# Spreading an expert's routing over more units, and placing its list matmuls one quarter later

## The chip, the cores and the metric

The kernel runs on one core of a Trainium2 chip. The metric is the time of one execution on the device in microseconds (us); the kernel before takes 2542.33 us, the median of three runs (2541.45 to 2545.57).

## What is computed

Two layers follow each other. The first is an attention without softmax over 8 batches of 2496 rows; the second is a mixture of 8 experts over all 19968 rows, where each row goes to one expert and each expert takes exactly 2496 rows.

```python
# attention, per batch: u, v of 2496 x 256, z of 2496 x 64
attn = np.maximum(scale * (z @ z.T), 0.0) ** 2
x = u * (attn @ v)
# mixture of experts over all rows of x
logits = x @ w_gate                      # 19968 x 8
for (token, expert) in the order of falling logits:
    if token is free and expert has under 2496 tokens: assign it
out[token] = relu(x[token] @ w1[expert]) @ w2[expert]
```

The greedy assignment is the part that the change touches. The kernel does it expert by expert: it finds the expert that fills first and the logit at which it is full (a search over thresholds), closes that expert, and goes on with the rest.

## The kernel before

The attention takes about the first 1490 us and is written in an order of its own; the change doesn't touch it. The rest is `moe`, whose order is that in which the program emits its instructions: each engine gets them as a list, and the framework's scheduler interleaves them by priority of emission and by the costs that it assumes.

The experts run one after the other. An expert's 2496 tokens are cut into five groups of up to 512, and the hidden width of 1024 into eight chunks of 128, so there are 8 x 5 x 8 = 320 steps. Step n emits the second layer of chunk n (`layer2`, twelve matmuls of 256 columns, lines L621 to L623) and the first layer of chunk n + 3 (`layer1`, six matmuls of up to 512 columns, L590 to L592). Each product of 32-bit numbers is made of three matmuls on high and low parts, so ScalarE makes the high part hh of the hidden chunk (L609) and VectorE the low part hl (L610). Weights are split in the same way (w1l and w2l, L510), and so are the tokens: they are gathered by GpSimd (L481), laid out through DRAM, transposed on VectorE (xt, L549) and split (xh on ScalarE, L553; xl on VectorE, L554).

While expert k - 1 computes, `route(k)` finds the tokens of expert k. It is a generator whose `yield`s carry weights ("units"), about 102 in sum for one routing, and `advance`, called twice a step (80 times per expert), draws as many units as the line with `YIELDS` wants; at the last call of an expert all that is left is drawn. So `YIELDS` sets how evenly the routing's instructions are spread among the matmuls of 40 steps.

A routing has these parts. The logits of the closed expert are shut and the best open expert of each row is found again (L69 to L91). Then come two searches of six rounds: VectorE compares all keys with up to seven thresholds (`mask`, L97), ten matmuls count them per expert (`srch`, L240), VectorE reduces the counts (hd L244, hr L246, hx L247), one matmul spreads them to all partitions (L323), VectorE picks the threshold (best L325, Dg L330, T L301, V L312) and makes the next mask. A last histogram with the mask fmask ends in L353. Then the ranks of the expert's tokens are made: running counts (cum, tot L376), a matmul over partitions (L388), rank and rj (L390 to L410). Last the list: for each quarter of 40 columns VectorE makes one-hot tiles (oa L420, hl L423 twice, and four ob tiles L429, which are queued behind the fourth last hl by `behind(4)`), and 40 matmuls of 40 columns each put the token numbers in place (L435; 36 in the last quarter). From the result VectorE makes idx (L440), the list that the gathers and the scatters of that expert use. The eighth expert takes what is left and has no search.

Of the kernel before, what the change touches and what calls it, by code (L numbers as in the profile page):

```python
# [21 lines left out]
def tile_attention_then_moe(ctx, tc, u, v, z, w_gate, w1, w2, out):  # L22
# [41 lines left out]

    attention(tc, u, v, z, w_gate, xd, identf, made, first, 1.0 / S)
    moe(tc, xd, first, jp, identf, w1, w2, out, B, S, consts, dram)


# [39 lines left out]
def moe(tc, xd, first, jp, identf, w1, w2, out, B, S, cp, dram):  # L108
    nc = tc.nc
# [3 lines left out]
    KT = NT + 1  # L113
# [3 lines left out]
    J = B * NT + B // 2  # L117
# [10 lines left out]
    ND = 15  # L128
    LA = 3
    AHEAD = 12  # L130
    YIELDS = 88
    with ExitStack() as ctx:
        rp = ctx.enter_context(tc.tile_pool(name="rp", bufs=1))
        wp = ctx.enter_context(tc.tile_pool(name="wp", bufs=3))
# [77 lines left out]
        CB = JP // 4  # L212
        QW = 4
# [5 lines left out]
        def by_quad(row, n):  # L219
            return row.rearrange("p (q r) -> p q r", r=QW)[:, :, None, :].to_broadcast([128, QN, n, QW])  # L220
# [9 lines left out]
        def srch():  # L230
            return ps.tile([128, 512], F32, name="srch")
# [20 lines left out]

        def behind(lag):
            return tc.issue_after(paced[-lag].ins) if len(paced) >= lag else nullcontext()

        def route(k):
            if k:
# [28 lines left out]
            else:  # L286
# [6 lines left out]
                for stage in range(2):  # L293
                    V = floor
                    for r, w in enumerate(widths):
                        n = (1 << w) - 1
# [24 lines left out]
                        p = srch()  # L321
# [29 lines left out]
                p = srch()  # L351
# [35 lines left out]
            p = srch()  # L387
# [25 lines left out]
            ROUTE[k]["idx"] = idx  # L413
            if k:
                p = srch()
                for c in range(0, JP, CB):
                    q = slice(c, c + CB)
                    oa = rp.tile([128, QN, KT, QW], BF, name="oa", bufs=2)
                    hl = rp.tile([128, QN, 2, KT, QW], BF, name="hl", bufs=2)
                    nc.vector.tensor_tensor(oa, by_quad(rab[:, 0, q], KT),  # L420
                                            slot[:, None, :KT].to_broadcast([128, QN, KT, QW]), op=OP.is_equal)
                    for i, d in enumerate((idh, idl)):
                        nc.vector.tensor_mul(hl[:, :, i], oa, by_quad(d[:, q], KT))  # L423
                    yield 1.5
                    ob = rp.tile([128, QN, 128, QW], BF, name="ob", bufs=4)
                    for b in range(0, 128, 32):
                        z = b + 32
                        with behind(4):
                            nc.vector.tensor_tensor(ob[:, :, b:z], by_quad(rab[:, 1, q], z - b),  # L429
                                                    slot[:, None, b:z].to_broadcast([128, QN, z - b, QW]),  # L430
                                                    op=OP.is_equal)
                        yield 1.5
                    for j in range(c, min(J, c + CB)):
                        n, r = divmod(j - c, QW)
                        nc.tensor.matmul(p[:, :2 * KT], ob[:, n, :, r], hl[:, n, :, :, r],  # L435
                                         start=(j == 0), stop=(j == J - 1))
                    yield
                idl_f = rp.tile([128, KT], F32, name="idl_f")
                nc.vector.tensor_copy(idl_f, p[:, KT:2 * KT])
                nc.vector.scalar_tensor_tensor(idx, p[:, :KT], 128.0, idl_f, op0=OP.mult, op1=OP.add)  # L440
                yield
                return
            both = [rp.tile([128, QN, 128, QW], BF, name="ob", bufs=4) for c in range(0, JP, CB)]
            for a0, a1 in ((0, 8), (8, 2 * KT)):
                na = a1 - a0
                p = srch()
                for c in range(0, JP, CB):
                    q = slice(c, c + CB)
                    ob = both[c // CB][:, :, :64]
                    hl = both[c // CB][:, :, 64:64 + 2 * na].rearrange("p q (i a) r -> p q i a r", i=2)  # L450
# [10 lines left out]
                    for j in range(c, min(J, c + CB)):  # L461
                        n, r = divmod(j - c, QW)
                        nc.tensor.matmul(p[:64, :2 * na], ob[:, n, :, r], hl[:, n, :, :, r],  # L463
                                         start=(j == 0), stop=(j == J - 1))
# [202 lines left out]
        for k in range(E):  # L667
# [13 lines left out]
            for h in range(2):  # L681
                at(n0 - 10 + h, split_w, k, 1, 0, h)
                at(n0 - 8 + h, split_w, k, 2, 0, h)
                at(n0 - 4 + h if k else -1, split_w, k, 1, 1, h)
                at(n0 - 2 + h if k else h, split_w, k, 2, 1, h)
        head = route(0)
        for mark in head:
            if mark == "listed":
                break
        N = len(seq)  # L690
        done = 0
        steps_k = {k: 0 for k in range(E)}
        gens = {k: route(k) for k in range(1, E)}

        def advance(pos):
# [4 lines left out]
            if pos < skip:  # L700
                return
            want = -(-(pos % (2 * PER) - skip + 1) * YIELDS // (2 * PER - skip))
            if (pos + 1) % (2 * PER) == 0:
# [406 lines left out]
```

## Time and profile before

| | |
|---|---|
| median of three runs | 2542.33 us (2541.45 to 2545.57) |
| profiled execution, its own time | 2541.26 us |
| its span | 2539.5 us |
| TensorE busy | 2445.5 us, 96% |
| VectorE busy | 1983.8 us, 78% |
| ScalarE busy | 1480.0 us, 58% |
| mean granted clock of TensorE | 0.977 |

The span is that of the profiled execution alone; its own time lies 1.07 us below the median. A line number in the profile is a line of the kernel above. PE is TensorE, DVE VectorE, ACT ScalarE, POOL GpSimd. In a group of instructions the last column is the idle time of the engine just before them, with the engines that ended it.

### The profile page before, as it was taken

The numbers are of one execution on the slowest core, as the hardware profiler recorded it, in microseconds if no ns is written. First come the engines' busy times: TensorE is split into PE (matmuls) and PEld (weight loads), VectorE is DVE, ScalarE is ACT, GpSimd is POOL, SyncE is SP. The second block draws the span as 40 slices with busy tenths as digits, with TensorE's granted clock in tenths as the row PEclk, the third lists the DMA queues.
The fourth block names the chain that finished last, engine by engine and source line by source line (L and its number), as shares of the span: only waits on it lengthen the run. The fifth ranks groups of instructions, "written<-read, shape, count | busy, mean of one in ns | idle before, by whom it ended". The sixth has DMA issues, their size and how long they took to land.

```text
span 2539.5 us, 67151 instructions
## 1 busy us (share of the span) xinstructions
PE 2445.5 (96%) x27913; PEld 2270.1 (89%) x27913; DVE 1983.8 (78%) x5653; ACT 1480.0 (58%) x1837; POOL 384.4 (15%) x747
## 2 busy tenths in 40 slices
PE   8999999999999999999999489999999999999998
PEld 7999999999999999999999377888888988898997
DVE  7888888888888988888877676979696968796332
ACT  7887888888887888888876022333333333333332
POOL 0000000000000000000000022423333233333331
PEclk9999999999999999999999578999999999999999
DMA  6031131121311311311100013332333232334320
GB/s 167 19 89 43 35 96 35 38 77 35 81 51 35 81 34 43 88 35 44 42 19 19 9 57 82 111 116 79 89 96 100 86 106 89 105 106 124 100 71 24
DMA packets 220705, 174.74 MB, mean 69 GB/s; under 512 B 167152, under 2 KB 188656, under 8 KB 220400
## 3 DMA queue, kind: packets, MB, share of 16 engines
q1 hardware_dynamic: 205296, 129.54, 18.1%
q0 software_dynamic: 15104, 40.91, 5.3%
q8 instruction: 218, 3.57, 0.6%
q14 instruction: 87, 0.71, 0.1%
HBM read 110.11 MB, written 60.29 MB: 67 GB/s over the span
## 4 chain that ended last, share of the span: by engine, by line
PE 86%; DVE 8%; issue 2%; DMA 1%; ACT 1%; POOL 1%; another core or an unknown queue 0%; SPq 0%; POOLq 0%; DVEq 0%; ACTq 0%
PE acc L927 43%; PE sc L856 11%; PE y L621 5%; PE y L623 5%; PE y L622 5%; PE hp L590 5%; PE hp L591 5%; PE hp L592 4%; PE srch L240 2%; PE srch L435 1%; DVE ob L429 1%; PE srch L463 1%; DVE mask L97 1%; POOL xg L481 1%; DMA wr<-in_moe_w_dram 0%
## 5 line engine op out<-in xcount | busy, mean ns | idle before, releaser
L927 PE MATMUL acc<-vh,hi 64*128 64x256 f32 x5280 | 744.7, 280 | 1.2 <-POOL seen L933 0.8
L927 PE MATMUL acc<-vl,hi 64*128 64x256 f32 x5280 | 740.9, 279 | 0.0
L927 PE MATMUL acc<-vh,lo 64*128 64x256 f32 x5016 | 709.4, 279 | 0.1
L877 DVE TENSOR_TENSOR lo<-a,hi 128x1024 fp32r<-128x1024 f32 (+3 forms) x400 | 457.3, 1143 | 103.6 <-ACT hi L869 102.8
L927 PEld LDWEIGHTS acc<-vh,hi 64*128 64x128 f32 x5280 | 502.0, 187 | 23.3 <-POOL seen L933 7.1
L609 ACT ACTIVATE hh<-hp 128x512 fp32r<-128x512 f32 (+1 forms) x320 | 186.9, 587 | 555.3 <-PE hp L592 429.0
L862 ACT ACTIVATE a<-sc 128x1024 f32<-128x1024 f32 (+1 forms) x400 | 400.1, 1000 | 178.5 <-PE sc L856 141.3
L927 PEld LDWEIGHTS acc<-vl,hi 64*128 64x128 f32 x5280 | 502.4, 187 | 0.0
L927 PEld LDWEIGHTS acc<-vh,lo 64*128 64x128 f32 x5016 | 477.5, 187 | 12.2 <-DVE lo L877 0.8
L963 DVE SCALAR_TENSOR_TENSOR lt<-xs,wgb 128x256 bf16<-128x256 f32 x1248 | 473.1, 421 | 1.4
L863 ACT ACTIVATE a<-a 128x1024 f32<-128x1024 f32 (+1 forms) x400 | 416.0, 1040 | 12.7
L621 PE MATMUL y<-w2h,hh 128*128 128x256 f32 (+1 forms) x1280 | 366.5, 286 | 2.3 <-ACT hh L609 1.9
L622 PE MATMUL y<-w2l,hh 128*128 128x256 f32 (+1 forms) x1280 | 363.4, 284 | 0.0
L869 ACT ACTIVATE hi<-a 128x1024 fp32r<-128x1024 f32 (+1 forms) x248 | 258.0, 1040 | 6.7
L590 PE MATMUL hp<-xh,w1h 128*128 128x512 f32 (+2 forms) x646 | 258.2, 402 | 3.6 <-ACT xh L583 1.6
L591 PE MATMUL hp<-xl,w1h 128*128 128x512 f32 (+2 forms) x646 | 254.0, 393 | 0.3 <-issue 0.3
L621 PEld LDWEIGHTS y<-w2h,hh 128*128 128x128 f32 (+1 forms) x1280 | 241.4, 189 | 13.1 <-ACT hh L609 2.4
L592 PE MATMUL hp<-xh,w1l 128*128 128x512 f32 (+2 forms) x646 | 250.0, 388 | 0.0
L622 PEld LDWEIGHTS y<-w2l,hh 128*128 128x128 f32 (+1 forms) x1280 | 241.4, 189 | 8.7
L933 POOL MEMSET seen<- 1x1 f32 x400 | 42.4, 106 | 1350.7 <-PE acc L927 1350.7
L653 POOL DMA_INDIRECT out_dram<-y,idx x160 | 173.1, 1082 | 383.9 <-ACT y L648 328.0
L481 POOL DMA_INDIRECT xg<-xd,idx x160 | 165.0, 1031 | 404.9 <-issue 110.3
(1162 smaller groups left out, 4055.7 us busy)
## 6 DMA issues: line engine op xcount, KB each, us to landing
vr<-in_v_dram SPq DMA_DIRECT2D x32, 512.0 KB
ur<-in_u_dram SPq DMA_DIRECT2D x32, 512.0 KB
xd<-xs SPq DMA_DIRECT2D x32, 512.0 KB
wr<-in_moe_w_dram SPq DMA_DIRECT2D x32, 512.0 KB
xgd<-xg SPq DMA_DIRECT2D x30, 512.0 KB
xg<-xgd SPq DMA_DIRECT2D x120, 128.0 KB
zw<-in_z_dram SPq DMA_DIRECT2D x112, 76.0 KB
xg<-xgd SPq DMA_DIRECT2D x32, 112.0 KB
```

The source lines that it names most:

```text
L590: nc.tensor.matmul(p[:, c], wh, xh, start=(d == 0), stop=False)
L591: nc.tensor.matmul(p[:, c], wh, xl, start=False, stop=False)
L592: nc.tensor.matmul(p[:, c], wl, xh, start=False, stop=(d == DH - 1))
L621: nc.tensor.matmul(o, h[:, c], wh, start=first, stop=False, skip_group_check=True)
L622: nc.tensor.matmul(o, h[:, c], wl, start=False, stop=False, skip_group_check=True)
L856: nc.tensor.matmul(P[s][:, t], x[b][r, k * 128:(k + 1) * 128], y[b][r, g * 512:g * 512 + w], start=(i == 0), stop=(i == 2))
L862: nc.scalar.activation(A[s], p, AF.Relu, scale=scale)
L863: nc.scalar.activation(A[s], A[s], AF.Square)
L869: nc.scalar.activation(HI[s], A[s], AF.Copy)
L877: nc.vector.tensor_sub(LO[s][:, :n], a[:, :n], h[:, :n].bitcast(F32))
L927: mm = nc.tensor.matmul(o, p, q, start=(kt == run == i == k == 0), stop=(last and k == 1), skip_group_check=True)
L963: nc.vector.scalar_tensor_tensor(t[r], XS[b, g][r, i], 1.0, WG["rows"][r, e], op0=OP.mult, op1=OP.mult, accum_out=lg[r, j, e:e + 1])
```

## The change

`YIELDS` goes from 88 to 96. The list matmuls of a quarter move into a function `place`, and are emitted only when the one-hot tiles of the next quarter have been; the last quarter's come after one more yield of 1.5 units. The number of instructions stays as it is.

```diff
--- before.py
+++ after.py
@@ -128,7 +128,7 @@
     ND = 15
     LA = 3
     AHEAD = 12
-    YIELDS = 88
+    YIELDS = 96
     with ExitStack() as ctx:
         rp = ctx.enter_context(tc.tile_pool(name="rp", bufs=1))
         wp = ctx.enter_context(tc.tile_pool(name="wp", bufs=3))
@@ -252,6 +252,12 @@
 
         def behind(lag):
             return tc.issue_after(paced[-lag].ins) if len(paced) >= lag else nullcontext()
+
+        def place(p, c, ob, hl):
+            for j in range(c, min(J, c + CB)):
+                n, r = divmod(j - c, QW)
+                nc.tensor.matmul(p[:, :2 * KT], ob[:, n, :, r], hl[:, n, :, :, r],
+                                 start=(j == 0), stop=(j == J - 1))
 
         def route(k):
             if k:
@@ -413,6 +419,7 @@
             ROUTE[k]["idx"] = idx
             if k:
                 p = srch()
+                ready = []
                 for c in range(0, JP, CB):
                     q = slice(c, c + CB)
                     oa = rp.tile([128, QN, KT, QW], BF, name="oa", bufs=2)
@@ -430,11 +437,12 @@
                                                     slot[:, None, b:z].to_broadcast([128, QN, z - b, QW]),
                                                     op=OP.is_equal)
                         yield 1.5
-                    for j in range(c, min(J, c + CB)):
-                        n, r = divmod(j - c, QW)
-                        nc.tensor.matmul(p[:, :2 * KT], ob[:, n, :, r], hl[:, n, :, :, r],
-                                         start=(j == 0), stop=(j == J - 1))
-                    yield
+                    ready.append((c, ob, hl))
+                    if len(ready) == 2:
+                        place(p, *ready.pop(0))
+                yield 1.5
+                place(p, *ready.pop(0))
+                yield
                 idl_f = rp.tile([128, KT], F32, name="idl_f")
                 nc.vector.tensor_copy(idl_f, p[:, KT:2 * KT])
                 nc.vector.scalar_tensor_tensor(idx, p[:, :KT], 128.0, idl_f, op0=OP.mult, op1=OP.add)
```

The lines behind the change shift: what is L323 before is L329 in the kernel after, L376 is L382, L429 is L436, L435 is L259 in `place`, L510 is L518, L590 to L592 are L598 to L600, L610 is L618, L621 to L623 are L629 to L631.

**The list on VectorE.** Here stands the start of the fourth expert's list in VectorE's row before (oa, ob and the list's hl are the one-hot tiles; hl__ with a number is a step's low part):

```order
L610 SCALAR_TENSOR_TENSOR hl__35317<-hp,hh 128x512
L420 TENSOR_TENSOR oa<-rab,slot 128x800
L429 TENSOR_TENSOR ob<-rab,slot 128x10x128
L423 TENSOR_TENSOR hl<-oa,idh 128x10x80
L423 TENSOR_TENSOR hl<-oa,idl 128x10x80
L610 SCALAR_TENSOR_TENSOR hl__35355<-hp,hh 128x512
L429 TENSOR_TENSOR ob<-rab,slot 128x10x128 x3
L610 SCALAR_TENSOR_TENSOR hl__35390<-hp,hh 128x512
L420 TENSOR_TENSOR oa<-rab,slot 128x800
L429 TENSOR_TENSOR ob<-rab,slot 128x10x128
L423 TENSOR_TENSOR hl<-oa,idh 128x10x80
L423 TENSOR_TENSOR hl<-oa,idl 128x10x80
```

And after:

```order
L427 TENSOR_TENSOR oa<-rab,slot 128x800
L618 SCALAR_TENSOR_TENSOR hl__35278<-hp,hh 128x512
L430 TENSOR_TENSOR hl<-oa,idh 128x10x80
L430 TENSOR_TENSOR hl<-oa,idl 128x10x80
L436 TENSOR_TENSOR ob<-rab,slot 128x10x128 x2
L618 SCALAR_TENSOR_TENSOR hl__35303<-hp,hh 128x512
L436 TENSOR_TENSOR ob<-rab,slot 128x10x128 x2
L427 TENSOR_TENSOR oa<-rab,slot 128x800
L618 SCALAR_TENSOR_TENSOR hl__35328<-hp,hh 128x512
L430 TENSOR_TENSOR hl<-oa,idh 128x10x80
L430 TENSOR_TENSOR hl<-oa,idl 128x10x80
L436 TENSOR_TENSOR ob<-rab,slot 128x10x128
```

The first oa now stands ahead of a low part, where it stood behind one, and the four ob tiles of the first quarter stand in two pairs with a low part between them, where one stood alone and three together.

**The first round of a search.** In VectorE's row of the fifth routing, from the first mask on, before:

```order
L97 TENSOR_TENSOR mask<-rep,at_28082 128x1120
L510 TENSOR_TENSOR w1l<-wr,w1h 128x512
L610 SCALAR_TENSOR_TENSOR hl__35969<-hp,hh 128x448
L510 TENSOR_TENSOR w1l<-wr,w1h 128x512
L244 TENSOR_TENSOR hd<-srch,diag 128x7x16
L246 TENSOR_REDUCE hr<-hd 128x7
L247 TENSOR_TENSOR hx<-hr,dE 128x8x7
L325 SCALAR_TENSOR_TENSOR best<-srch,step_28074 128x8x7
L330 TENSOR_REDUCE Dg<-best 128x1
L610 SCALAR_TENSOR_TENSOR hl__36009<-hp,hh 128x448
L301 TENSOR_TENSOR T<-next_28084,Dg 128x7
L312 TENSOR_TENSOR V<-floor,Dg 128x1
```

After:

```order
L97 TENSOR_TENSOR mask<-rep,at_28082 128x1120
L618 SCALAR_TENSOR_TENSOR hl__35884<-hp,hh 128x448
L618 SCALAR_TENSOR_TENSOR hl__35933<-hp,hh 128x448
L518 TENSOR_TENSOR w1l<-wr,w1h 128x512
L618 SCALAR_TENSOR_TENSOR hl__35969<-hp,hh 128x448
L244 TENSOR_TENSOR hd<-srch,diag 128x7x16
L518 TENSOR_TENSOR w1l<-wr,w1h 128x512
L246 TENSOR_REDUCE hr<-hd 128x7
L247 TENSOR_TENSOR hx<-hr,dE 128x8x7
L331 SCALAR_TENSOR_TENSOR best<-srch,step_28074 128x8x7
L336 TENSOR_REDUCE Dg<-best 128x1
L618 SCALAR_TENSOR_TENSOR hl__36019<-hp,hh 128x448
```

The mask stands two low parts earlier, one of the two w1l stands between hd and hr instead of before hd, and the low part between Dg and T is a later one.

On TensorE, the same place, from the last of the ten histogram matmuls to L323, before:

```order
L240 MATMUL srch<-mask,oh 128x112
L590 MATMUL hp<-xh_35659,w1h 128x448
L591 MATMUL hp<-xl_35660,w1h 128x448
L592 MATMUL hp<-xh_35659,w1l 128x448
L590 MATMUL hp<-xh_35782,w1h 128x448
L591 MATMUL hp<-xl_35783,w1h 128x448
L592 MATMUL hp<-xh_35782,w1l 128x448
L323 MATMUL srch<-hx,onesr 128x64
```

And after, the last matmuls in front of what is now L329 (the twelve matmuls of a second layer, of which these are the last two, stand between them and the histogram):

```order
L630 MATMUL y_35944<-w2l,hh 64x256
L631 MATMUL y_35944<-w2h,hl__35884 64x256
L598 MATMUL hp<-xh_35672,w1h 128x448
L599 MATMUL hp<-xl_35673,w1h 128x448
L600 MATMUL hp<-xh_35672,w1l 128x448
L598 MATMUL hp<-xh_35782,w1h 128x448
L599 MATMUL hp<-xl_35783,w1h 128x448
L600 MATMUL hp<-xh_35782,w1l 128x448
L329 MATMUL srch<-hx,onesr 128x64
```

Between the histogram and the matmul that spreads the counts there were six matmuls of a first layer, and now there are those six and twelve of a second layer.

**The last routing.** VectorE's row of the eighth expert's routing, from the selection of its tokens to the offsets that L388's result gives, before:

```order
L367 TENSOR_SCALAR sel<-asg,cstar 128x160
L510 TENSOR_TENSOR w1l<-wr,w1h 128x512
L371 SCALAR_TENSOR_TENSOR cum<-ones_j,sel 128x160
L610 SCALAR_TENSOR_TENSOR hl__39576<-hp,hh 128x448
L376 CAST tot<-cum 128x1
L510 TENSOR_TENSOR w1l<-wr,w1h 128x512
L390 TENSOR_SCALAR off<-srch 128x1
```

After:

```order
L373 TENSOR_SCALAR sel<-asg,cstar 128x160
L377 SCALAR_TENSOR_TENSOR cum<-ones_j,sel 128x160
L618 SCALAR_TENSOR_TENSOR hl__39460<-hp,hh 128x448
L382 CAST tot<-cum 128x1
L618 SCALAR_TENSOR_TENSOR hl__39509<-hp,hh 128x448
L518 TENSOR_TENSOR w1l<-wr,w1h 128x512
L618 SCALAR_TENSOR_TENSOR hl__39576<-hp,hh 128x448
L396 TENSOR_SCALAR off<-srch 128x1
```

The running count tot stands two low parts earlier, and in front of the w1l instead of behind one.

## Rows read from the trace of the kernel before

**Rows 1.** The page: busy time by engine, and the clock row of the 40 slices.

```profile
PE 2445.5 (96%) x27913; PEld 2270.1 (89%) x27913; DVE 1983.8 (78%) x5653; ACT 1480.0 (58%) x1837; POOL 384.4 (15%) x747
...
PEclk9999999999999999999999578999999999999999
```

**Rows 2.** TensorE's groups, 1530 to 2540 us; last column idle time before, with its releasers.

```profile
L435 PE MATMUL srch<-hl,ob 128*128 128x40 bf16 x1092 | 48.9, 214 | 0.0
...
L240 PE MATMUL srch<-mask,oh 128*128 128x112 bf16 (+1 forms) x710 | 41.9, 205 | 7.2 <-DVE mask L97 6.1 <-issue 0.9
L323 PE MATMUL srch<-hx,onesr 128*128 128x64 f32 (+1 forms) x71 | 15.2, 213 | 8.0 <-DVE hr L246 3.6 <-DVE hx L247 3.6
...
L353 PE MATMUL srch<-hx,onesr 128*128 128x16 f32 x6 | 1.4, 235 | 1.7 <-DVE hr L246 0.9 <-DVE hx L247 0.8
```

**Rows 3.** The same view, 1620 to 1712 us (routing of the second expert).

```profile
L240 PE MATMUL srch<-mask,oh 128*128 128x112 bf16 (+1 forms) x120 | 7.0, 204 | 1.4 <-issue 0.9 <-DVE mask L97 0.2
L323 PE MATMUL srch<-hx,onesr 128*128 128x64 f32 (+1 forms) x12 | 2.5, 209 | 1.6 <-DVE hx L247 1.5
```

**Rows 4.** The same view, 1742 to 1845 us (routing of the third expert).

```profile
L240 PE MATMUL srch<-mask,oh 128*128 128x112 bf16 (+1 forms) x120 | 7.0, 204 | 1.6 <-DVE mask L97 1.6
L323 PE MATMUL srch<-hx,onesr 128*128 128x64 f32 (+1 forms) x12 | 2.7, 221 | 2.3 <-DVE hr L246 1.2 <-DVE hx L247 0.9
```

**Rows 5.** The same view, 2005 to 2105 us (routing of the fifth expert).

```profile
L240 PE MATMUL srch<-mask,oh 128*128 128x112 bf16 (+1 forms) x120 | 7.0, 204 | 1.3 <-DVE mask L97 1.3
L323 PE MATMUL srch<-hx,onesr 128*128 128x64 f32 (+1 forms) x12 | 2.4, 202 | 1.3 <-DVE hx L247 1.2
```

**Rows 6.** Timeline, 1563 to 1569 us: start, duration, engine, line, operation, idle before.

```profile
1563.11 0.67 PE L240 MATMUL srch<-mask,oh 128*128 128x112 bf16 x10
...
1563.59 0.36 PE L621 MATMUL y<-w2h,hh 128*128 128x256 f32 x1
...
1564.03 0.28 PE L621 MATMUL y<-w2h,hh 128*128 128x256 f32 x1
...
1564.39 0.40 PE L590 MATMUL hp<-xh,w1h 128*128 128x512 f32 x1
...
1564.45 0.22 DVE L247 TENSOR_TENSOR hx<-hr,dE 128x56 fp32r<-128x56 f32 x1
...
1564.62 0.40 PE L591 MATMUL hp<-xl,w1h 128*128 128x512 f32 x1
...
1564.86 0.22 PE L323 MATMUL srch<-hx,onesr 128*128 128x64 f32 x1
...
1565.82 0.83 DVE L97 TENSOR_TENSOR mask<-rep,T 128x1120 bf16<-128x1120 int16 x1
...
1566.70 0.67 PE L240 MATMUL srch<-mask,oh 128*128 128x112 bf16 x10
...
1566.82 0.69 DVE L610 SCALAR_TENSOR_TENSOR hl__29736<-hp,hh 128x512 fp32r<-128x512 f32 x1
```

**Rows 7.** The same view, 2019 to 2023.5 us (a first round).

```profile
2021.02 1.06 DVE L510 TENSOR_TENSOR w1l<-wr,w1h 128x512 fp32r<-128x512 f32 x1
...
2022.61 0.22 DVE L247 TENSOR_TENSOR hx<-hr,dE 128x56 fp32r<-128x56 f32 x1
2022.88 0.30 PE L323 MATMUL srch<-hx,onesr 128*128 128x64 f32 x1 [1.22 <-DVE hx L247]
```

**Rows 8.** VectorE's groups, 1530 to 2540 us.

```profile
L549 DVE STREAM_TRANSPOSE xt<-xg 128x512 f32<-128x512 f32 (+1 forms) x76 | 52.6, 692 | 0.4
```

**Rows 9.** TensorE's waits, 2265 to 2340 us: total, times, longest.

```profile
PE hp L590 <- ACT xh L553: 1.3, 1, 1.3
PE srch L388 <- issue: 0.9, 1, 0.9
```

**Rows 10.** Windows: length, busy time of each engine, granted clock, DMA share, GB/s.

```profile
2292.00:2296.00 4.00, 3.31 (x46) 2.86 (x47) 4.00 (x8) 2.77 (x4) 0.94 (x1) 0.82 0.44 120
2296.00:2300.00 4.00, 4.00 (x20) 3.54 (x20) 2.18 (x4) 0.60 (x1) 3.08 (x4) 0.75 0.46 117
```

## The prediction

> **What bounds the kernel now.** I read the page first. TensorE is busy 2445.5 us of a span of 2539.5, and the clock row is at full speed but for the hand-over between the two halves [rows 1]. The second half, from about 1490 us, is where the change lies. So I grouped TensorE's instructions there by line, from 1530 us to 2540 us: the reader is to look at the last column, the idle time in front of each group. The list matmuls L435, which the change moves, waited 0.0 us in 1092 instructions. The search waits: 7.2 us before the histograms L240, 8.0 before L323, 1.7 before L353 [rows 2]. The rest is small. So all that an order of emission can win there is about 20 us, 0.8% of the time, and most of it is the search's chain between VectorE and TensorE, six times over (the eighth expert is found without a search).
>
> Then the same view per routing: the second expert's search loses 1.4 + 1.6 us [rows 3], the third's 1.6 + 2.3 [rows 4], the fifth's 1.3 + 1.3 [rows 5]. With 0.3 each for L353 these are 3.3, 4.2 and 2.9. Of the total of 16.9 that leaves 6.5 for the first, fourth and sixth searches. The fourth and sixth have the same order of instructions as the fifth, so they take about 2.9 each and the first about 0.7.
>
> Last the timeline of one round that stands clear [rows 6]: L240 starts at 1563.11, VectorE's hx at 1564.45 is ready for L323 at 1564.86, the next mask starts at 1565.82 and its histogram at 1566.70. L240 itself takes TensorE 0.48 (the next matmul starts at 1563.59). So TensorE needs some 1.2 us of other matmuls between a histogram and L323 (1564.86 less 1563.11 is 1.75, less the 0.48, less a little slack), and some 1.7 between L323 and the next histogram (1.84 less L323's own 0.06 and slack), or it waits. I call the matmul work that stands there the cover, counted from the order at 0.12 us per 256-column and 0.23 per 512-column matmul (1564.03, 1564.39, 1564.62: three spacings of the one, then one of the other). A foreign VectorE instruction inside the chain adds its own time: hl 0.69 [rows 6], a transpose xt 0.69 [rows 8], a w1l 1.06 [rows 7].
>
> **The change part by part.** (a) It removes and adds no instruction on any engine: 0.
>
> (b) The list matmuls stand later against VectorE's one-hot tiles. They waited 0.0 before [rows 2], so nothing can be won there. The last quarter still stands where it stood in TensorE's order, so the token list and the gathers behind it come no earlier either: 0. What changes is the slot of everything else: at 96 units the routing is spread more evenly, about 6 of its 102 units are left for the last call instead of 15, and VectorE takes up the list and the next search two to three steps (2.84 us each) sooner.
>
> (c) The first routing keeps its order up to the list: 0.
>
> (d) Routings 4, 5 and 6, alike. First round: VectorE had two w1l in front of hd, the second from 2021.02 to 2022.08, so hx came at 2022.61 and L323 waited 1.22 [rows 7] behind a cover of 1.23. Afterwards 18 matmuls stand there instead of 6 (cover 2.66), and the mask is issued two steps earlier; one w1l stays between hd and hr. Chain 1.2 + 1.06 + some 0.5 of an hl in front is 2.8 against 2.66: 0.2 stays of 1.2, so -1.0. Second round: the next mask is queued behind an hl half a step ahead, the need is 1.7 + 0.69 = 2.4, and the cover falls from 2.66 to 2.04: +0.5 (0.4 and a late start). In the eighth round an xt (0.69) is now in a chain with cover 2.13, against 1.2 + 0.69 = 1.9, where the cover was 2.83 before: between 0 and 0.7, taken as +0.3. In the twelfth, an hl and an xt (1.38) against the same 2.13: 2.6 less 2.13, +0.4. The other rounds lose or gain 0.1 to 1.5 us of cover, most of them without falling below the need; the third, fourth and ninth rounds, fmask's histogram and L353 together I put at +0.6, bounded by -0.4 (all hold) and +1.4 (each 0.3 late). Sum +0.8 per routing; three of them +2.4. The bounds: -1.8 per routing if only 1.1 of the 2.9 stays, +3.2 if every hl that stands in a chain is late.
>
> (e) Routing 2: the 1.4 at the first histogram stays, since VectorE is still full there. The L323 that stood with no cover waited 1.5 of the 1.6 [rows 3]; it gets a cover. As in (d) about 0.7 comes new in other rounds: -0.8.
>
> (f) Routing 3: the first round as in (d) and its L323 waits of 2.3 [rows 4] go down by 1.4; the second mask adds 0.5: -0.9.
>
> (g) Routing 8, the last, has two waits of TensorE, 0.9 at L388 and 1.3 at the first matmul of a new block of rows, which waits for xh [rows 9]. The running count tot had a w1l (1.06) and an hl in front of it; afterwards its w1l stands behind, and the transpose for xh is one step (2.84 us) earlier in VectorE's row. Both waits are shorter than these shifts: -0.9 and -1.3. Behind the second wait the granted clock was 0.82 and then 0.75 for 4 us each [rows 10], at full speed before. The work lost is (0.18 + 0.25) x 4 = 1.7 us, and it goes with the waits: -1.7. Nothing is late next there, since the last routing has no search behind it. If the transposes' data land late instead, 0 of the 3.9.
>
> A rule that speaks against this reading is weighed here. The row shows a granted clock that stayed at full speed through waits of 1.2 us and more in the searches, as before L323 [rows 7], and fell only at the last routing. The Trainium skill's page "TensorE: Matmul & The Clock Gate", in "HAM oscillation — how this bites in real kernels", says that the gate falls back to its low rate over gaps in which TensorE waits, and that the price is paid again at each gap; by it, new waits close together in three searches would each cost clock as well. That is rival D below.
>
> Sum: 0 + 0 + 0 + 2.4 - 0.8 - 0.9 - 3.9 = -3.2 us. The profiled execution took 2541.26 us and lies 1.1 us below the median of the runs shown, 2542.33. 2541.3 - 3.2 is 2538.1, and in the median's frame **2539.1 us**.
>
> **The rivals.** A, faster: VectorE's lead of two to three steps covers the rounds of (d) as well, so that hl's are done before the masks fall due. For it: the whole loss of (d) hangs on foreign instructions that stand in the chain by issue order, and an instruction that was issued early and done early costs nothing. Against it: VectorE's hl can't run before ScalarE and TensorE have made its input, whatever its lead. Then each of three routings wins 1.0 instead of losing 0.8: 5.4 less, **2533.7**.
>
> B, no gain at the end: in the last routing the row block lands late by its DMAs, not by VectorE, and 0.9 + 1.3 + 1.7 = 3.9 stay. For it: the first wait reads as issue, not as VectorE [rows 9]. **2543.0**.
>
> C, slower: the half-step lead with which the hl's now stand in front of masks and hd makes VectorE wait in order for TensorE's next layer-1 matmul at about six places of a search, 0.4 us more each than I gave, in routings 3 to 6: 6 x 0.4 x 4 = 9.6, **2548.7**. For it: VectorE takes its row in order, and a mask behind an hl can't pass it. Against it: five rounds of the old order stand so already, and the fifth routing lost 2.9 in all [rows 5]. It decides from 2.1 us more per routing on (8.3 to the bound of slower, in four).
>
> D, the clock: what the last routing shows, 1.7 us of lost work behind two waits [rows 9, 10], happens in four searches: 6.8 more, **2545.9**. Against it: the waits of before, of like length, cost no clock.
>
> That the change does nothing is no rival, since the order on VectorE and TensorE moves in six of seven routings; that gains and losses cancel lies within the likeliest case's own range.
>
> **How the numbers follow.** The forecast has 0.50 (its own range 2536.5 to 2542.0), A 0.22, B 0.15, C 0.10, D 0.03. A measurement of this kernel can tell about 0.2%, 5.1 us: faster is below 2537.2, slower above 2547.4. Faster: A's 0.22 and about a quarter of the forecast's half, 0.12: 0.34. Slower: C's 0.10 and the upper ends of D and B, 0.02: 0.12. The rest, 0.54, is no difference. The range goes from 2533.0, a little below A, to 2546.5, above B and D; what is left out is C, some 0.1, and A's lower half, under 0.1.
>
> **What would show it.** In the changed kernel: list matmuls still without idle time; the first L323 of routings 4 to 6 with 0.3 us or less in place of 1.22; 0.3 to 0.7 us at the second histogram of each of them; 3.5 to 4 us of search waits in each; no wait at L388 and none at the xh block in the last routing, and a clock at full speed through it. Searches that lose under 2 us each speak for A, a clock still at 0.75 in the last routing for B, 5 us or more each for C. The forecast is wrong if the search's idle time of the second half (16.9 us now) comes out under 15 or over 20, or if anything outside these seven routings moves.

## The result, and the profile after

The kernel after takes 2561.67 us (median of four runs, 2556.9 to 2564.07), the kernel before 2541.89 on the same chip: a ratio of 1.0077 [1.0059, 1.0095]. It is slower by 19.8 us, where 3.2 us faster was forecast. The profiled execution took 2560.87 us, span 2559.1, which is 19.6 us over that of before. The page, lines as in [rows 1]:

```profile
PE 2450.8 (96%) x27913; PEld 2268.6 (89%) x27913; DVE 1979.8 (77%) x5653; ACT 1480.0 (58%) x1837; POOL 379.7 (15%) x747
...
PEclk9999999999999999999999579999999999999999
```

The work is the same and the page shows almost nothing. TensorE's groups from 1530 to 2560 us show it (as [rows 2]; the last column is the idle time before, with its releasers):

```profile
L259 PE MATMUL srch<-hl,ob 128*128 128x40 bf16 x1092 | 48.9, 213 | 0.7 <-DVE ob L436 0.7
...
L240 PE MATMUL srch<-mask,oh 128*128 128x112 bf16 (+1 forms) x710 | 42.1, 205 | 18.0 <-DVE mask L97 16.3 <-issue 1.4
L329 PE MATMUL srch<-hx,onesr 128*128 128x64 f32 (+1 forms) x71 | 16.3, 229 | 13.3 <-DVE hx L247 5.5 <-DVE hr L246 5.5 <-DVE hd L244 1.6
```

The list matmuls still wait for almost nothing (0.7 us). The histograms wait 18.0 us instead of 7.2, the matmul that spreads the counts (L329) 13.3 instead of 8.0. Over all lines TensorE idles 37.5 us there, against 22.3 before.

Step by step (the start of the first second-layer matmul with hl of each step, after less before), the 19.6 us fall on these routings. The prediction's routings 2 to 6 are `route(2)` to `route(6)`; its "routing 8, the last" is `route(7)`.

| | attention and start of the experts | 2 | 3 | 4 | 5 | 6 | last |
|---|---|---|---|---|---|---|---|
| forecast, us | 0 | -0.8 | -0.9 | +0.8 | +0.8 | +0.8 | -3.9 |
| measured, us | +0.1 | +8.3 | +0.5 | +4.3 | +4.3 | +3.2 | -1.0 |

The clock has moved too. Windows of after (TensorE busy, ..., granted clock, DMA share, GB/s):

```profile
1656.00:1660.00 4.00, 3.51 (x25) 3.40 (x26) 2.70 (x12) 0.60 (x1) 0.00 (x0) 0.63 0.39 134
1660.00:1664.00 4.00, 4.00 (x32) 3.39 (x32) 2.25 (x9) 0.60 (x1) 0.00 (x0) 0.94 0.73 133
...
1960.00:1964.00 4.00, 3.73 (x25) 3.54 (x26) 1.89 (x7) 0.00 (x0) 0.00 (x0) 0.60 0.53 119
...
2316.00:2320.00 4.00, 4.00 (x26) 3.54 (x25) 3.50 (x6) 2.31 (x5) 2.69 (x4) 1.00 0.62 142
```

In two searches the clock was at its lower level for a part of 4 us, (0.37 + 0.06) x 4 = 1.7 us and 0.40 x 4 = 1.6 us of lost work; in the last routing, where [rows 10] had 0.82 and 0.75, it stayed at full speed. The idle time (15.2 us more) and the clock (3.3 us lost, where before lost 1.7) make 16.8 of the 19.6 us; the rest isn't placed.

**Where a wait comes from.** The longest wait is in routing 2. Timeline of after (start, duration, engine, line, operation, idle before and its releaser):

```profile
1649.28 1.00 POOL L661 DMA_INDIRECT out_dram<-y,idx  x1 [0.31 <-issue]
...
1650.57 0.67 PE L240 MATMUL srch<-mask,oh 128*128 128x112 bf16 x10
1650.59 0.92 POOL L661 DMA_INDIRECT out_dram<-y,idx  x1 [0.30 <-ACT hh L617]
...
1651.81 0.98 POOL L489 DMA_INDIRECT xg<-xd,idx  x1 [0.31 <-issue]
...
1652.04 0.39 PE L599 MATMUL hp<-xl,w1h 128*128 128x512 f32 x1
1653.10 0.96 POOL L489 DMA_INDIRECT xg<-xd,idx  x1 [0.30 <-issue]
1655.51 0.27 DVE L244 TENSOR_TENSOR hd<-srch,diag 128x112 f32<-128x112 f32 x1 [4.49 <-remote]
...
1656.49 0.27 PE L329 MATMUL srch<-hx,onesr 128*128 128x64 f32 x1 [4.06 <-DVE hx L247]
```

The reader is to see that VectorE's hd, which needs only the ten histogram matmuls of 1650.57 to 1651.24, starts at 1655.51, though VectorE stood idle for 4.49 us. In the bare round of [rows 6] the whole way from histogram to hx takes 1.3 us. TensorE had run its row up to L329 and idled 4.06 us. GpSimd meanwhile sent indirect DMAs (scatters L661, gathers L489) with 0.3 us between them. The same in routing 5, in the tenth round:

```profile
2088.98 0.67 PE L240 MATMUL srch<-mask,oh 128*128 128x112 bf16 x10
2089.20 0.97 POOL L661 DMA_INDIRECT out_dram<-y,idx  x1 [0.30 <-issue]
...
2090.47 0.99 POOL L489 DMA_INDIRECT xg<-xd,idx  x1 [0.30 <-issue]
2090.68 0.39 PE L600 MATMUL hp<-xh,w1l 128*128 128x512 f32 x1
...
2091.77 0.92 POOL L489 DMA_INDIRECT xg<-xd,idx  x1 [0.30 <-issue]
...
2092.29 0.28 DVE L244 TENSOR_TENSOR hd<-srch,diag 128x112 f32<-128x112 f32 x1 [2.97 <-PE hp L600]
...
2093.27 0.27 PE L329 MATMUL srch<-hx,onesr 128*128 128x64 f32 x1 [0.78 <-DVE hr L246]
...
2093.80 0.60 ACT L617 ACTIVATE hh<-hp 128x512 fp32r<-128x512 f32 x1 [5.20 <-PE srch L329]
...
2096.27 0.42 PE L240 MATMUL srch<-mask,oh 128*128 128x48 bf16 x10 [1.25 <-DVE mask L97]
```

hd comes 2.6 us after its histogram's end, and ScalarE's relu hh, whose last matmul is L600 at 2090.68, starts at 2093.80 after an idle 5.20. So two engines wait for results that TensorE has long computed by the trace. (The Trainium skill's "Perfetto Trace Analysis", section "Tensor Engine Instruction (MATMUL, LD_WEIGHTS)", says that a matmul's end in a profile is estimated, and that its semaphore goes out only when PSUM has acknowledged the writes. The rows agree that the one doesn't tell the other; how many microseconds can lie between them is in these rows alone.)

The trace also keeps the times at which semaphores were raised. TensorE's counter, for which hd waits, was raised at 1655.48 in the first case and at 2092.26 in the second, and hd starts 0.02 us behind it in both. In the median it is raised 0.01 us behind the modelled end of its matmul. So the waiting engine isn't slow to see it: the counter itself goes up late.

I then counted this over the whole second half: a step of the experts is late where hh starts over 0.6 us after its last matmul could have ended and ScalarE was free. Of about 320 steps 24 are late before, 25 after, nearly all of them beside indirect DMAs sent back to back. (The count moves by up to some six with the end that one takes for a matmul.) The kernel before has it in [rows 4] as well: the 1.6 us at a histogram there is one wait, of 1.63 us at 1818.46, behind a round whose histogram stood at 1808.89 and whose hd came like this:

```profile
1812.65 0.27 DVE L244 TENSOR_TENSOR hd<-srch,diag 128x112 f32<-128x112 f32 x1 [2.51 <-PE hp L592]
```

An expert's 40 steps have two chains of eight indirect DMAs, four scatters and four gathers, some 10 us each, at steps 10 to 13 and 35 to 38, and some six chains of four. A late hh costs little: the first layer is three steps ahead. A search round has no such slack: what is late in it, TensorE waits for.

The same can be counted in the searches alone: hd and best are the two VectorE instructions of a round that take a result of TensorE, some 150 from 1540 us on. Lateness here is the start less the end of the matmul, or less the time when VectorE came free if that was later. While no indirect DMA runs, none is over 0.2 us late, in either kernel. While some run, 13 of 79 are over 0.4 us late before, 11.8 us in sum, and 18 of 60 after, 31.4 us. So the change puts fewer results beside indirect DMAs, not more, but those that it puts there are later. TensorE's waits in the searches split in the same way: those in front of which an hd, a best or an hh was that late (since the search's last matmul) rise from 6.3 us to 20.8, and all others go from 10.4 to 9.4.

### The profile page after: what moved, and what is told of

Its sections match the earlier page's. It is cut to its first block, busy times and chain, and to the rows that moved or that the text cites. A ratio compares the mean times of both kernels' runs of the same rounds, so it can differ in the third digit from the quotient of the medians.

```text
span 2559.1 us, 67144 instructions
## 1 busy us (share of the span) xinstructions
PE 2450.8 (96%) x27913; PEld 2268.6 (89%) x27913; DVE 1979.8 (77%) x5653; ACT 1480.0 (58%) x1837; POOL 379.7 (15%) x747
## 4 chain that ended last, share of the span: by engine, by line
PE 89%; DVE 6%; issue 2%; ACT 1%; DMA 1%; POOL 1%; another core or an unknown queue 0%; SPq 0%; POOLq 0%; DVEq 0%; ACTq 0%
PE acc L935 43%; PE sc L864 11%; PE y L629 5%; PE hp L600 5%; PE y L631 5%; PE hp L598 5%; PE hp L599 5%; PE y L630 5%; PE srch L259 2%; PE srch L240 2%; PE srch L471 1%; DVE mask L97 1%; PE srch L329 1%; DVE w1l L518 1%; POOL xg L489 0%
## 5 line engine op out<-in xcount | busy, mean ns | idle before, releaser
L629 PE MATMUL y<-w2h,hh 128*128 128x256 f32 (+1 forms) x1280 | 368.3, 288 | 0.3 <-ACT y L656 0.3
L598 PE MATMUL hp<-xh,w1h 128*128 128x512 f32 (+2 forms) x646 | 256.0, 398 | 4.7 <-issue 3.0
L629 PEld LDWEIGHTS y<-w2h,hh 128*128 128x128 f32 (+1 forms) x1280 | 241.5, 189 | 10.3 <-ACT y L656 0.5
L600 PE MATMUL hp<-xh,w1l 128*128 128x512 f32 (+2 forms) x646 | 250.5, 388 | 0.0
L489 POOL DMA_INDIRECT xg<-xd,idx x160 | 161.9, 1012 | 453.8 <-issue 109.5
L661 POOL DMA_INDIRECT out_dram<-y,idx x160 | 170.8, 1068 | 358.9 <-ACT y L656 288.3
```

Source lines behind the costliest of these rows:

```text
L598: nc.tensor.matmul(p[:, c], wh, xh, start=(d == 0), stop=False)
L600: nc.tensor.matmul(p[:, c], wl, xh, start=False, stop=(d == DH - 1))
L629: nc.tensor.matmul(o, h[:, c], wh, start=first, stop=False, skip_group_check=True)
```

## Experiments

The theory: TensorE's results reach the other engines 1 to 4 us late while GpSimd sends indirect DMAs back to back, and the change has moved search rounds into such stretches (in routings 3 to 6 the tenth, and the first or second). By the count above this second half holds only in part: other rounds are hit, and harder, but not more of them. The rival is C of the prediction, as a matter of row order: VectorE's low parts and w1l stand ahead of masks and hd. It predicts that the loss stays whatever GpSimd does. A second one is that the loss comes from one half of the change, the order of the list matmuls or the 96 units. Ratios are to the kernel before on the same chip, in each block of runs; it took 2549.53 us in the first block, 2541.63 in the second, 2541.16, 2521.19 and 2541.15 in the others. Only rows of one block are compared.

**First block: one half of the change, and no indirect DMAs.** `y96` is before with one line changed, `place88` is after with that line changed back:

```diff
-    YIELDS = 88        # y96
+    YIELDS = 96
-    YIELDS = 96        # place88
+    YIELDS = 88
```

> Only YIELDS goes from 88 to 96; the list matmuls are emitted as before. Two theories of the 19.6 us. Late signals: VectorE and ScalarE get TensorE's completion signals 1 to 4 us late in certain stretches in which GpSimd issues indirect DMAs (24 of 320 first-layer steps in the kernel before, 25 after), and the change has moved two rounds of each search into such stretches. Row order: the new waits come from low parts that stand before masks and hd in VectorE's row, and the late signals are a by-product. By both, the place of the search rounds is set mostly by YIELDS, so 12 to 20 us slower than before (2554 to 2562); if the list's placement does it, within 3 us of before.

> Only the list matmuls are emitted one quarter later; YIELDS stays 88. By late signals the rounds stay nearly where they were against the indirect DMAs: within 5 us of before (2537 to 2547). By row order the low parts ahead of the first masks move a little: 0 to 8 us slower.

Measured: `y96` 2574.07, 1.0092 [1.0071, 1.0112]; `place88` 2566.08, 1.006 [1.0044, 1.0077]. Both miss what was expected: `y96` is 24.5 us slower and not 12 to 20, `place88` 16.5 and not at most 8, by either theory. Each half alone is slower, so the loss doesn't belong to one of them, and they don't add up. In `y96` the histograms wait 19.3 us and L323 17.9, with 27 late steps; in `place88` 14.6 and 10.0, with 28, and its clock falls in three more places (from 1764, 2012 and 2348), 8.5 us of work.

`plain` replaces every gather and scatter, in both kernels:

```diff
-                gather(t[:n, i], xd, idx[:n, 4 * g + i:4 * g + i + 1])
+                r = S * k + 512 * g + 128 * i
+                nc.sync.dma_start(t[:n, i], xd[r:r + n, :])
...
-                st = nc.gpsimd.indirect_dma_start(
-                    out=out, out_offset=bass.IndirectOffsetOnAxis(ap=idx[:n, a:a + 1], axis=0),
-                    in_=y[:n, i], in_offset=None)
+                r = S * k + 128 * a
+                st = nc.sync.dma_start(out[r:r + n, :], y[:n, i])
```

> The kernel before, with each indirect gather and scatter of 128 rows replaced by an ordinary DMA of 128 consecutive rows from SyncE (so the rows of x that an expert takes, and where its results go, are not those of the routing). Late signals: no first-layer step has its relu more than 0.6 us late after its matmul (24 before), and the time falls by 1 to 5 us. Row order: the late steps stay, time within 3 us of before.

> The changed kernel with the same replacement as plain_before. Late signals: the difference from plain_before is at most 6 us instead of 19.6, and the waits before the second and the eleventh round's next matmul (0.7 to 2.3 us each) are gone. Row order: it stays 15 to 20 us slower than plain_before.

Measured: `plain_before` 2497.31, 0.9789 [0.9772, 0.9805]; `plain_after` 2500.05, 0.9799 [0.9783, 0.9815]. TensorE's groups, of `plain_before`:

```profile
L240 PE MATMUL srch<-mask,oh 128*128 128x112 bf16 (+1 forms) x697 | 40.5, 203 | 2.0 <-DVE mask L97 1.7
L323 PE MATMUL srch<-hx,onesr 128*128 128x64 f32 (+1 forms) x70 | 14.9, 213 | 3.2 <-DVE hx L247 2.9
```

and of `plain_after`:

```profile
L240 PE MATMUL srch<-mask,oh 128*128 128x112 bf16 (+1 forms) x700 | 40.7, 204 | 0.9 <-DVE mask L97 0.6
L329 PE MATMUL srch<-hx,onesr 128*128 128x64 f32 (+1 forms) x70 | 15.0, 214 | 4.4 <-DVE hx L247 4.2
```

Of the 19.8 us of loss 2.7 are left, and no step is late in either. How much faster they are in all (52 us for `plain_before`, where 1 to 5 were expected) says less, since the gathers no longer wait for the list either, and the first expert starts earlier.

This doesn't refute row order by itself, because the scheduler has placed the instructions anew. Of the 72 stretches of VectorE's row that begin with a mask, 61 differ between `plain_after` and after, mostly in where a transpose, an xl or an hl stands; in `pscat_after` below it is 36 and in `pause_after` 60, though the expectation of the latter counts on an unchanged row. Row order alone falls by the trace of after: VectorE's order can make VectorE late, but it can't leave it idle for 4.49 us in front of an hd that lacks nothing but TensorE's counter, and where no result is late the searches wait no longer than before (9.4 us, 10.4 before).

**Second block: the scatters alone, and another emission.** `pscat` makes only the second of these two edits.

> The same in the kernel before. Late signals: at most 8 late steps, within 6 us of pscat_after. Row order: 15 to 20 us faster than pscat_after.

> The changed kernel with only the scatters of results replaced by ordinary DMAs to consecutive rows (results go to wrong rows); the indirect gathers stay, and so does what they wait for. Late signals come with indirect DMAs of either kind, most where many follow each other: at most 8 late steps instead of 25, and a span near that of plain_after plus what the routing's list holds up: under 2535. If it was the gathers' wait for the list that made the difference in plain_after, the time stays above 2550.

Measured, one run each: 2513.71 and 2516.38, again 2.7 apart, with 7 and 10 late steps (at most 8 were expected) and search waits of 8.8 and 8.5 us (L240 and the spreading matmul). Single runs don't settle a difference of 2.7. With gathers alone the chains are half as long, and most of the lateness is gone.

`spread` keeps all indirect DMAs, but emits the four of a gather or of a scatter in four steps, one in each:

```diff
+                    for i in range(4):
+                        at(n0 - AHEAD + i, gather_x, k, g, (i,))
...
+                    for i in range(4):
+                        at(n0 + FT - 1 + i, send_y, k, g, (i,))
```

> The kernel before with each group's four gathers and four scatters emitted one per step instead of four at once (the same work, and the layout of gathered rows two steps later). If signals are late where indirect DMAs follow each other without a pause, half of the 24 late steps go and the time falls by 2 to 12 us. If a single indirect DMA is enough, the late steps are as many, elsewhere, and the time is within 5 us or worse.

> The changed kernel with the same spreading. By the same reasoning 8 to 25 us faster than the changed kernel, so between 10 us faster and 10 us slower than before; with row order as the cause it stays 12 us or more slower than spread_before.

A miss: 2544.88, 1.0012 [1.0002, 1.0021], and 2564.05, 1.0092 [1.0075, 1.0108]. GpSimd still ran them back to back, because a gather starts when its buffer comes free and not when it is emitted (at 2064.31 in `spread_after` the first waits 4.31 us for the transposes xt, and three follow 0.30 apart), and 27 and 28 steps were late. It tells nothing about pauses.

**Third block: pauses between indirect DMAs.** Everything is kept, and behind each indirect DMA GpSimd clears a small tile three times:

```diff
+        def paused(issue):
+            with tc.issue_after(rest[-1].ins) if rest else nullcontext():
+                st = issue()
+            for _ in range(3):
+                with tc.issue_after(st.ins if _ == 0 else rest[-1].ins):
+                    rest.append(nc.gpsimd.memset(idle, 0.0))
+            return st
```

> The changed kernel with three small memsets on GpSimd (128x256 of a scratch tile) behind each indirect DMA, so that the unbroken chains of eight indirect DMAs (four scatters and four gathers in some 10 us, twice in an expert's 40 steps) get pauses of half a us or more between them. If completion signals are late because indirect DMAs follow each other without a pause: under 10 late steps instead of 25 and a time within 6 us of the kernel before. If each indirect DMA does it by itself: as many late steps, spread further, within 5 us of the changed kernel or slower. Row order: the memsets touch nothing on VectorE and TensorE, within 3 us of the changed kernel.

> The kernel before with the same memsets. Pauses help: 3 to 12 us faster than before, since its 24 late steps go as well. Each DMA by itself: within 5 us or slower. Row order: within 3 us of before.

Measured: `pause_after` 2532.97, 0.997 [0.9958, 0.9981]; `pause_before` 2542.07, 1.0006 [0.9996, 1.0015]. Late steps: 3 and 4. The change that costs 19.8 us without pauses gains 9.1 with them. In `pause_after` the searches wait little and the list not at all:

```profile
L259 PE MATMUL srch<-hl,ob 128*128 128x40 bf16 x1092 | 49.0, 213 | 0.0
L240 PE MATMUL srch<-mask,oh 128*128 128x112 bf16 (+1 forms) x710 | 41.4, 204 | 2.5 <-DVE mask L97 2.3
L329 PE MATMUL srch<-hx,onesr 128*128 128x64 f32 (+1 forms) x72 | 16.3, 226 | 5.8 <-DVE hx L247 4.8
```

In `pause_before` the searches wait as little, but two other places take it back, so that the 3 to 12 us that were expected didn't come:

```profile
L435 PE MATMUL srch<-hl,ob 128*128 128x40 bf16 x1092 | 48.7, 213 | 4.7 <-DVE ob L429 4.7
...
L240 PE MATMUL srch<-mask,oh 128*128 128x112 bf16 (+1 forms) x710 | 41.9, 205 | 3.3 <-DVE mask L97 3.1
L323 PE MATMUL srch<-hx,onesr 128*128 128x64 f32 (+1 forms) x71 | 14.8, 208 | 3.0 <-DVE hx L247 2.9
...
L388 PE MATMUL srch<-tot,tri 128*128 128x2 bf16 (+1 forms) x7 | 1.2, 176 | 3.2 <-DVE tot L376 1.6 <-DVE left L384 1.5
```

Here the list matmuls wait for their one-hot tiles, which those of the kernel after don't, and the clock fell at 1636 to 1648 and at 1720 to 1728. So what the change does to the list is worth something, once nothing else hides it; which half of the change does it isn't separated.

**Fourth block: how long a pause.** One memset in place of three, and two.

> The changed kernel with one memset of 0.32 us behind each indirect DMA in place of three. If any break in the chain is enough: late steps under 8 and a time within 4 us of pause_after, 8 us under before. If the rate of indirect DMAs counts (one per 1.3 us without, 1.6 us with one memset, 2.3 us with three): 10 to 20 late steps, and a time between the changed kernel's and pause_after's.

> The same with two memsets (0.64 us). Any break: within 4 us of pause_after. Rate: fewer late steps than with one, and a time at or a little above pause_after's.

Measured: 2524.49, 1.0013 [1.0004, 1.0023], and 2528.45, 1.0027 [1.0015, 1.0038], with 1 and 3 late steps. On this chip the kernel before took 2521.19, some 20 us less than on the others. There is no trace of before from it, so whether its results come late there isn't shown. Both runs are a little slower than before there, where the first alternative had one memset 8 us under it. The shorter the pause, the faster.

**Fifth block: the same four on one chip.** `before2` and `after2` are the two kernels again, `pause_after2` and `pause1_after2` have three memsets and one.

> The kernel before again, for a trace from the same chip as the next three. Its median was 2521 to 2550 us on five chips. If late signals make that difference, their count and the idle time of TensorE in the searches go with the time: about 24 late steps and 17 us at 2541, under 10 late steps and under 10 us of idle time near 2521.

> The changed kernel on that chip. Late signals: 15 to 25 us slower than before where before shows some 24 late steps; where before shows under 10 (a chip near 2521), within 8 us of it. Row order: 15 to 20 us slower on every chip.

> The changed kernel with three memsets behind each indirect DMA. Late signals: at most 4 late steps on any chip, and 15 us or more under the changed kernel where that has late steps.

> The changed kernel with one memset behind each indirect DMA. If any break is enough, within 4 us of pause_after2 with at most 4 late steps on a chip where the changed kernel has some 25; if the rate counts, 5 us or more above it.

| | us | ratio | late steps | histograms, spreading matmul, us idle |
|---|---|---|---|---|
| `before2` | 2539.55 | 0.999 [0.9981, 1.0] | 20 | 6.9, 8.7 |
| `after2` | 2563.0 | 1.0078 [1.0062, 1.0095] | 32 | 15.4, 15.3 |
| `pause_after2` (median of six executions) | 2534.47 | 0.9971 [0.9959, 0.9983] | – | – |
| `pause1_after2` | 2526.94 | 0.9933 [0.9915, 0.9951] | 7 | 5.0, 6.9 |

One memset of 0.33 us behind each indirect DMA makes the kernel after 36 us faster, and 13 us faster than `before2`. It is 7.5 us under three memsets with 7 late steps, which neither alternative foresaw: any break was to give the same time with at most 4, and a rate was to make it slower. GpSimd's groups in `pause1_after2`:

```profile
L672 POOL DMA_INDIRECT out_dram<-y,idx x157 | 174.5, 1112 | 464.8 <-ACT y L667 444.4 <-issue 19.4 <-ACT hh L628 0.5
...
L496 POOL MEMSET idle<- 128x256 f32 x306 | 101.0, 330 | 0.2
```

Of the 36 us, 23.0 are TensorE's idle time from 1530 us on (37.5 to 14.5). Another 7.9 are clock: `after2` was under 0.95 of full speed in eight windows of 4 us, at 1532 to 1544, 1656 to 1664, 2036 to 2044 and 2316 to 2320, and `pause1_after2` in none before its last matmuls. The last 5 I can't place.

## Why the prediction was wrong

**The step that failed is the price of a round**, in (d) and (e). The prediction took a round from the timeline of a bare one [rows 6], "1.2 us of other matmuls between a histogram and L323", and weighed covers by order alone. That holds only if VectorE gets TensorE's result when the matmul ends. In after hd came up to 4.27 us later than that. Whether the rest of the sum would have come out as a gain isn't shown: the change costs 2.7 us in `plain` and gains 9.1 with three memsets, both with other rows of VectorE.

(a) and (b): no work was added, and the list waits 0.7 us instead of 0.0. Right, but not the whole: with the pauses the old placement of the list waits 4.7 us and the new one 0.0, so a gain that (b) denied exists where nothing else covers the list.

(c): +0.1 us by the first routing, right.

(d), forecast +0.8 each, measured +4.3, +4.3 and +3.2. The first L329 of routing 5 waits 1.05 us (at 2035.83) where 0.2 was forecast, and 1.06 to 1.09 in `pause1_after2`, so this wait is none of lateness. VectorE's row in after shows it, with TensorE's L329 at its end:

```profile
2032.58 1.07 DVE L518 TENSOR_TENSOR w1l<-wr,w1h 128x512 fp32r<-128x512 f32 x1 [2.34 <-ACT w1h L516]
...
2034.29 1.05 DVE L518 TENSOR_TENSOR w1l<-wr,w1h 128x512 fp32r<-128x512 f32 x1
...
2035.83 0.30 PE L329 MATMUL srch<-hx,onesr 128*128 128x64 f32 x1 [1.05 <-DVE hx L247]
```

Both w1l stand in the chain, because the first had to wait for ScalarE's w1h; the prediction counted one of them, so the gain of 1.0 was never there. The second histogram, forecast +0.5 by a half-step hl, waits 2.31 us at 2040.55, behind a best that came 2.27 us late; in `pause1_after2` it waits for nothing. Another 1.07 at 2065.35 stands behind a best that was 1.10 late, and 0.78 + 1.25 in and behind the tenth round shown above; the prediction gave these nothing. All search waits of routing 5 are 6.5 us, where (d) leaves 3.7; in `pause1_after2` they are 1.09 + 0.60 + 0.36 = 2.05. That is the side of rival A, as far as its somewhat different order can tell.

(e), forecast -0.8, measured +8.3: 4.06 at 1656.49 with 1.7 of clock behind it, and 1.62 + 1.27 in another late round, from 1690.97 on, are 8.65; against that 2.1 us of old waits went, and the first histogram waits 0.9 more. The prediction misread [rows 3] there: the 1.4 is all histograms of the routing, and the first had 0.87 (at 1637.30), which is 1.80 in after. This is the largest error, and it is one histogram in the middle of a chain of scatters and gathers.

(f), forecast -0.9, measured +0.5: the same kind, small.

(g), forecast -0.9 -1.3 -1.7. The wait at L388 has gone and the clock is at full speed, so the first and the third came. The third is luck: on the chip of the fifth block it is the other way, with full speed in `before2` and 0.58 from 2316 to 2320 in `after2`. The wait for the new row block didn't go; it is in three pieces, of TensorE in after:

```profile
2311.86 0.49 PE L598 MATMUL hp<-xh,w1h 128*128 128x512 f32 x1 [0.91 <-ACT xh L561]
2312.78 0.50 PE L599 MATMUL hp<-xl,w1h 128*128 128x512 f32 x1 [0.43 <-DVE xl L562]
2314.86 0.50 PE L598 MATMUL hp<-xh,w1h 128*128 128x512 f32 x1 [0.77 <-ACT xh L561]
```

2.1 us instead of 1.3, net -1.0 by the steps.

The rivals. C had the side and a size of +9.6, but its mechanism alone isn't what cost: where no result is late the searches wait no longer than before. It has a share in four waits of 1.25 to 1.27 at the eleventh histogram, where an hl stands in front of the mask and its hh is 2.7 to 3.6 us late. A's mechanism, VectorE's lead covering the rounds, is in part what the pauses uncover, though not in the first round: its 2533.7 was 8.6 under before, and `pause_after` is 8.2 under. That the sizes agree is chance, since the pauses also take away waits that before had. D was taken for unlikely because "the waits of before, of like length, cost no clock"; but the longest of the new ones, 4.06 us, had no like before. The clock fell behind it, and behind 1.98 us at 1960, and not behind 2.31 us at 2040; in `after2` it fell there as well, behind 2.44. B was right that the wait for rows stays, and wrong on L388 and on the clock.

What would have told it beforehand stood in the trace of before: 24 steps whose hh started late beside an idle ScalarE, and a hd, in the round ahead of the wait in [rows 4], that came 3.1 us after its histogram's end while GpSimd sent gathers. I read the idle time of TensorE alone, and there the lateness showed only as 1.6 us.

**What stays open.** Why results are late in a stretch of indirect DMAs: the trace shows that TensorE's counter is raised late and that the waiting engine follows at once, not whether the matmul's write is late as well or its signal alone. Why a pause of 0.33 us is enough isn't shown, nor why one place is late in one routing and prompt in the next: the same round of before was prompt in routings 4 to 6, and late there in `place88`. The change also alters GpSimd's own order: in the chain at steps 10 to 13 the four scatters come first before, and behind two gathers after, in routings 3 to 6. That order isn't separated from the place of the rounds, and part of the effect of the pauses may lie in it, since they fix it; it isn't needed for lateness, which is there in `place88` with the scatters first (2.6 us at 1953.78). How much of the difference between chips comes from this isn't known.

## What to carry to other kernels

Before pricing a chain between two engines by its order, compare the start of each waiting instruction with the end of what it waits for, over the whole trace: where an idle engine starts late, the price of a round depends on what other engines do in that stretch. A search or another chain without slack belongs outside the stretches in which GpSimd sends indirect DMAs back to back, or these are to be set apart. Moving work by a few steps, even with no instruction added, is then worth as much as what it collides with. And an experiment that alters one engine's instructions can alter the order on all of them: compare the rows before calling the order unchanged.

## What the runs showed of the hardware

While GpSimd sent indirect DMAs with 0.3 us between them, results of TensorE reached VectorE and ScalarE up to 4.3 us late (hd at 1655.51 after matmuls that ended at 1651.24), and it was the raising of TensorE's counter that came late (1655.48). In none of the 17 traces was an hd or a best after 1540 us over 0.2 us late while no indirect DMA ran. With one 0.33 us memset behind each, the late steps went from 32 to 7 and the time fell by 36 us; with three, no hd or best was over 0.4 us late. With ordinary DMAs in their place, from SyncE, none of some 320 steps was late. And the same kernel took 2521 us on one chip and 2550 on another, more than the change is worth, so only runs on one chip were compared.
